# Layer scale on one core: five loads instead of seven, and partitions that own 64 consecutive rows of each half of the tensors

## The chip, the cores and the metric

One core of a Trainium2 chip runs the kernel; the other cores do nothing. The metric is the device time of one execution in microseconds. Executions of one kernel agree within some tenths of a per cent, so the differences of 0.3 us in this study need repeated runs; where a ratio is given, it comes from rounds in which both kernels ran on the same chip (five rounds for each experiment, four to six runs of the kernel in question). All runs quoted were at a granted clock of 1.0.

## The reference

```python
B, S, D = 1024, 16, 512          # x, y: bf16 [1024, 16, 512]; gamma: bf16 [512]
def reference(x, y, gamma):
    return x + gamma * y
```

Flattened, x and y have 16384 rows of 512 bf16, 1 KiB a row and 16 MiB a tensor. Two are read and one is written: 50.33 MB.

## The kernel before

With 128 partitions each partition owns 128 rows. "Row" below means one such row index: 1 KiB in each of 128 partitions, 128 KiB in all. SyncE issues the loads, ScalarE issues gamma and the stores, one small matmul on TensorE spreads gamma over the partitions, VectorE multiplies by gamma and adds x. The kernel keeps all 128 rows of y on chip, but only 77 rows of x, so the last x loads reuse the buffer of rows already added.

```python
PIECES = [40, 37, 40, 11]        # VectorE's pieces, in rows
# loads: (tensor, first row, last row, place in the x buffer); stores 's' of rows 0..64 and 64..128
SP = [('x', 0, 40, 0), ('y', 0, 40), ('x', 40, 77, 40), ('y', 40, 77), ('y', 77, 128),
      ('x', 77, 117, 0), ('x', 117, 128, 40)]
ACT = [('g',), ('s', 0, 64), ('s', 64, 128)]
RELEASE = ('x', 77, 117, 0)      # the stores wait until this load has landed
DVE = [('m', 0), ('a', 0), ('m', 1), ('a', 1), ('m', 2), ('a', 2), ('m', 3), ('a', 3)]
# ... (cut)
xv = xf.rearrange("(p n) d -> p n d", p=P)     # partition p owns rows p*128 .. p*128+127
# ... (cut) in the loop over SP: an x load waits until the adds that read its buffer are done
if need > known:
    eng.wait_ge(s_add, need)
to = x_sb[:, w[3] : w[3] + w[2] - w[1], :]
i = eng.dma_start(out=to, in_=xv[:, w[1] : w[2], :]).then_inc(s_load[w], 16)
# ... (cut) VectorE, per piece c
nc.vector.tensor_tensor(out=yt, in0=yt, in1=g, op=MULT).then_inc(s_dve, 1)
nc.vector.tensor_tensor(out=yt, in0=xt, in1=yt, op=ADD).then_inc(s_add, 1)
```

Of the kernel before, what the change touches and what calls it, by code (L numbers as in the profile page):

```python
# [3 lines left out]


PIECES = [40, 37, 40, 11]



SP = [('x', 0, 40, 0), ('y', 0, 40), ('x', 40, 77, 40), ('y', 40, 77), ('y', 77, 128), ('x', 77, 117, 0), ('x', 117, 128, 40)]  # L10
ACT = [('g',), ('s', 0, 64), ('s', 64, 128)]

EARLY = (2, 1)


RELEASE = ('x', 77, 117, 0)

DVE = [('m', 0), ('a', 0), ('m', 1), ('a', 1), ('m', 2), ('a', 2), ('m', 3), ('a', 3)]
MULT, ADD = mybir.AluOpType.mult, mybir.AluOpType.add


def _take(sem, n, eng):


    return eng.wait_ge(sem, n).then_inc(sem, -n)  # L25


def kernel(
    tc: tile.TileContext,
    x: bass.AP,  # L30
    y: bass.AP,
    gamma: bass.AP,
    out: bass.AP,
):



    nc = tc.nc
    P = nc.NUM_PARTITIONS
    tc.close()  # L40
    tc.compile()  # L41

    xf = x.flatten_outer_dims()
    yf = y.flatten_outer_dims()
    of = out.flatten_outer_dims()
    N, D = xf.shape
    rows = N // P
    n = len(PIECES)
    assert sum(PIECES) == rows
    starts = [sum(PIECES[:c]) for c in range(n + 1)]  # L50
    dt = xf.dtype
    xv = xf.rearrange("(p n) d -> p n d", p=P)
    yv = yf.rearrange("(p n) d -> p n d", p=P)
    ov = of.rearrange("(p n) d -> p n d", p=P)

    gamma_row = nc.alloc_sbuf_tensor("gamma_row", [1, D], dt).ap()
    ones_row = nc.alloc_sbuf_tensor("ones_row", [1, P], dt).ap()
    gamma_sb = nc.alloc_sbuf_tensor("gamma_sb", [P, D], dt).ap()
    y_sb = nc.alloc_sbuf_tensor("y_sb", [P, rows, D], dt).ap()
    x_loads = [w for w in SP + ACT if w[0] == "x"]  # L60
    y_loads = [w for w in SP + ACT if w[0] == "y"]
    stores = [w for w in SP + ACT if w[0] == "s"]
    for loads in (x_loads, y_loads, stores):
        assert sum(w[2] - w[1] for w in loads) == rows
    x_rows = max(w[3] + w[2] - w[1] for w in x_loads)
    x_sb = nc.alloc_sbuf_tensor("x_sb", [P, x_rows, D], dt).ap()
    gamma_ps = nc.alloc_psum_tensor("gamma_ps", [P, D], mybir.dt.float32).ap()

    sem = nc.alloc_semaphore
    s_gamma, s_ones, s_ps, s_dve = sem("s_gamma"), sem("s_ones"), sem("s_ps"), sem("s_dve")  # L70
    s_load = {w: sem("s_" + "_".join(map(str, w[:2]))) for w in x_loads + y_loads}
    s_add, s_go, s_rel, s_end, s_out = sem("s_add"), sem("s_go"), sem("s_rel"), sem("s_end"), sem("s_out")
    added = [a for kind, *a in DVE if kind == "a"]
    order = {a[0]: k for k, a in enumerate(added)}

    def meets(a, b, c, d):
        return a < d and c < b

    def pieces_of(a, b):
        return [c for c in range(n) if meets(starts[c], starts[c + 1], a, b)]  # L80

    def x_at(row):
        return next(w[3] + row - w[1] for w in x_loads if w[1] <= row < w[2])

    def frees(w):

        old = x_loads[: x_loads.index(w)]
        old = [v for v in old if meets(v[3], v[3] + v[2] - v[1], w[3], w[3] + w[2] - w[1])]
        return [c for v in old for c in pieces_of(v[1], v[2])]

    early = []

    def ring(eng, what, n_early):

        known, went = 0, False
        for k, w in enumerate(what):
            kind = w[0]
            need = frees(w) if kind == "x" else pieces_of(w[1], w[2]) + list(w[3:]) if kind == "s" else []
            need = max((order[c] + 1 for c in need), default=0)
            if kind == "s" and not went:  # L100
                _take(s_go, 1, eng)
                went = True
            if need > known:
                eng.wait_ge(s_add, need)
                known = need
            if kind == "g":
                i = eng.dma_start(out=gamma_row, in_=gamma.unsqueeze(0)).then_inc(s_gamma, 16)
            elif kind == "x":
                to = x_sb[:, w[3] : w[3] + w[2] - w[1], :]
                i = eng.dma_start(out=to, in_=xv[:, w[1] : w[2], :]).then_inc(s_load[w], 16)  # L110
            elif kind == "y":
                r = slice(w[1], w[2])
                i = eng.dma_start(out=y_sb[:, r, :], in_=yv[:, r, :]).then_inc(s_load[w], 16)
            else:
                r = slice(w[1], w[2])
                i = eng.dma_start(out=ov[:, r, :], in_=y_sb[:, r, :]).then_inc(s_out, 16)
            if k < n_early:
                early.append(i.ins)

    ring(nc.sync, SP, EARLY[0])  # L120
    ring(nc.scalar, ACT, EARLY[1])


    nc.vector.memset(ones_row, 1.0).then_inc(s_ones, 1)  # L124
    _take(s_ones, 1, nc.tensor)
    _take(s_gamma, 16, nc.tensor)
    nc.tensor.matmul(gamma_ps, ones_row, gamma_row, start=True, stop=True).then_inc(s_ps, 1)  # L127
    _take(s_ps, 1, nc.vector)
    nc.vector.tensor_copy(out=gamma_sb, in_=gamma_ps).then_inc(s_dve, 1)  # L129
    _take(s_dve, 1, nc.vector)  # L130

    _take(s_load[RELEASE], 16, nc.tensor)
    nc.tensor.sem_inc(s_go, 1)
    nc.tensor.sem_inc(s_rel, 1)

    landed, open_mults = set(), 0

    def need(loads, c):
        for w in loads:
            if w not in landed and meets(starts[c], starts[c + 1], w[1], w[2]):  # L140
                if w == RELEASE:
                    _take(s_rel, 1, nc.vector)
                else:
                    _take(s_load[w], 16, nc.vector)
                landed.add(w)

    for kind, *args in DVE:
        c = args[0]
        yt = y_sb[:, starts[c] : starts[c + 1], :]
        if kind == "m":  # L150
            need(y_loads, c)
            g = gamma_sb[:, None, :].to_broadcast([P, PIECES[c], D])
            nc.vector.tensor_tensor(out=yt, in0=yt, in1=g, op=MULT).then_inc(s_dve, 1)  # L153
            open_mults += 1
        else:
            need(x_loads, c)
            if open_mults:
                _take(s_dve, open_mults, nc.vector)
                open_mults = 0
            at = x_at(starts[c])  # L160
            xt = x_sb[:, at : at + PIECES[c], :]
            nc.vector.tensor_tensor(out=yt, in0=xt, in1=yt, op=ADD).then_inc(s_add, 1)  # L162


    nc.scalar.sem_inc(s_end, 1)
    _take(s_end, 1, nc.sync)
    _take(s_add, n, nc.sync)
    _take(s_out, 16 * len(stores), nc.sync)

    main = nc.main_func.blocks[0].instructions  # L170
    names = {i.name for i in early}
    for b in nc.main_func.blocks[1:]:
        for i in [i for i in b.instructions if i.name in names]:
            b.instructions.remove(i)
    for k, i in enumerate(early):
        main.insert(1 + k, i)
# [30 lines left out]
```

## Time and profile before

| | before |
|---|---|
| time, median | 119.99 us (119.98 to 120.29) |
| span in the trace | 118.8 us |
| VectorE busy | 70.2 us (59%) |
| the two DMA queues, share of 16 engines | 66.0% + 32.6% |
| last add ends / second store issued / its first packet | 97.44 / 97.47 / 98.47 us |

The span counts from the first instruction to the last event; the timed run has 1.3 us more around it. (The trace of before is of an execution of 120.14 us, 118.8 of them span; the 1.2 us in the prediction come from setting that span against the median of 119.99.) A DMA of 128 partitions is cut into 128 packets, one a partition, 8 on each of the 16 DMA engines, and each engine ends with a 4-byte packet that counts up the semaphore (145 packets under 512 B on the page: 9 DMAs x 16, and one for gamma). The packet records of the trace give start and duration of each. The lines that carry the reading are in the prediction.

### The profile page before, as it was taken

How to read it: one execution, taken by the hardware profiler on the slowest of the kernel's cores; microseconds unless marked ns; L12 is line 12 of the kernel's file. 1: busy time of each engine (PE TensorE's matmuls, PEld its weight loads, DVE VectorE, ACT ScalarE, POOL GpSimd, SP SyncE). 2: the span in 40 equal slices, each digit the busy share in tenths (PEclk: the TensorE clock that was granted, in tenths of full speed). 3: DMA queues.
4: the chain of work that ended last, by engine and by line, in shares of the span. 5: the costliest groups of instructions: out<-in, count | busy, mean ns of one | idle time of the engine just before them, and what ended most of it. 6: DMA issues, size and time to landing. Idle time of an engine off the chain costs nothing. (4 is left out here: it accounts for less than half of the span.)

```text
span 118.8 us, 84 instructions
## 1 busy us (share of the span) xinstructions
PE 0.6 (0%) x1; PEld 0.1 (0%) x1; DVE 70.2 (59%) x10; POOL 0.2 (0%) x4
## 2 busy tenths in 40 slices
PE   0100000000000000000000000000000000000000
PEld 0000000000000000000000000000000000000000
DVE  0020000009999999799999999999999980000000
POOL 0000000000000000000000000000000000000000
DMA  7999999999999999989696999998899889988890
GB/s 221 442 441 441 441 441 441 441 425 408 408 421 472 485 459 408 475 369 563 281 563 262 441 414 441 408 637 353 353 530 530 353 353 397 662 353 353 353 684 22
DMA packets 1298, 50.33 MB, mean 424 GB/s; under 512 B 145, under 2 KB 146, under 8 KB 146
## 3 DMA queue, kind: packets, MB, share of 16 engines
q1 hardware_dynamic: 1008, 33.55, 66.0%
q10 hardware_dynamic: 290, 16.78, 32.6%
HBM read 33.56 MB, written 16.78 MB: 424 GB/s over the span
## 5 line engine op out<-in xcount | busy, mean ns | idle before, releaser
L153 DVE TENSOR_TENSOR y_sb<-y_sb,gamma_sb 128x20480 bf16<-128x20480 bf16 (+2 forms) x4 | 34.8, 8688 | 20.6 <-DVEq L25 20.6
L162 DVE TENSOR_TENSOR y_sb<-x_sb,y_sb 128x20480 bf16<-128x20480 bf16 (+2 forms) x4 | 34.8, 8691 | 0.6
L129 DVE CAST gamma_sb<-gamma_ps 128x512 bf16<-128x512 f32 x1 | 0.7, 690 | 4.1 <-DVEq L25 4.1
L124 DVE MEMSET ones_row<- 1x128 bf16 x1 | 0.2, 165 | 2.0 <-PEq L41 2.0
L127 PE MATMUL gamma_ps<-gamma_row,ones_row 1*128 1x512 bf16 x1 | 0.6, 581 | 5.5 <-PEq L25 5.5
L127 PEld LDWEIGHTS gamma_ps<-gamma_row,ones_row 1*128 1x128 bf16 x1 | 0.1, 98 | 5.5 <-issue 5.5
L191 POOL MEMSET const-bfloat16-1.0<- 128x1 bf16 x1 | 0.1, 102 | 0.0
L191 POOL MEMSET const-uint8-127<- 128x1 uint8 x1 | 0.1, 101 | 0.0
L191 POOL MEMSET const-float32-0.0<- 128x1 f32 x1 | 0.1, 99 | 0.2 <-issue 0.2
L191 POOL MEMSET const-float32-1.0<- 128x1 f32 x1 | 0.1, 98 | 0.0
## 6 DMA issues: line engine op xcount, KB each, us to landing
x_sb<-in_x_dram SPq DMA_DIRECT2D x2, 5120.0 KB, 21.3
y_sb<-in_y_dram SPq DMA_DIRECT2D x1, 6528.0 KB, 61.8
y_sb<-in_y_dram SPq DMA_DIRECT2D x1, 5120.0 KB, 26.3
x_sb<-in_x_dram SPq DMA_DIRECT2D x1, 4736.0 KB, 36.0
y_sb<-in_y_dram SPq DMA_DIRECT2D x1, 4736.0 KB, 46.9
x_sb<-in_x_dram SPq DMA_DIRECT2D x1, 1408.0 KB, 10.6
out_dram<-y_sb ACTq DMA_DIRECT2D x2, 21.8
gamma_row<-in_gamma_dram ACTq DMA_DIRECT2D x1, 1.0 KB
```

The lines of the kernel that those rows point to most:

```text
L124: nc.vector.memset(ones_row, 1.0).then_inc(s_ones, 1)
L127: nc.tensor.matmul(gamma_ps, ones_row, gamma_row, start=True, stop=True).then_inc(s_ps, 1)
L129: nc.vector.tensor_copy(out=gamma_sb, in_=gamma_ps).then_inc(s_dve, 1)
L153: nc.vector.tensor_tensor(out=yt, in0=yt, in1=g, op=MULT).then_inc(s_dve, 1)
L162: nc.vector.tensor_tensor(out=yt, in0=xt, in1=yt, op=ADD).then_inc(s_add, 1)
L191: nc = _bacc.Bacc("TRN2", target_bir_lowering=False, num_devices=1)
```

## The change

Intent: each full load covers 8 MiB of contiguous memory, there are two loads fewer, and VectorE is done earlier, so that the last store can be issued earlier. Core of the diff:

```diff
-PIECES = [40, 37, 40, 11]
+PIECES = [53, 11, 53, 11]
-SP = [('x', 0, 40, 0), ('y', 0, 40), ('x', 40, 77, 40), ('y', 40, 77), ('y', 77, 128), ('x', 77, 117, 0), ('x', 117, 128, 40)]
+SP = [('y', 0, 64), ('x', 0, 64, 0), ('y', 64, 128), ('x', 64, 117, 0), ('x', 117, 128, 64)]
-RELEASE = ('x', 77, 117, 0)
+RELEASE = ('x', 64, 117, 0)
-DVE = [('m', 0), ('a', 0), ('m', 1), ('a', 1), ('m', 2), ('a', 2), ('m', 3), ('a', 3)]
+DVE = [('m', 0), ('m', 1), ('a', 0), ('a', 1), ('m', 2), ('m', 3), ('a', 2), ('a', 3)]
-    xv = xf.rearrange("(p n) d -> p n d", p=P)
+    xv = xf.rearrange("(c p n) d -> p c n d", p=P, c=2)
     # the same for yv and ov; at(v, a, b) picks the half c and the rows in it
-                i = eng.dma_start(out=to, in_=xv[:, w[1] : w[2], :]).then_inc(s_load[w], 16)
+                i = eng.dma_start(out=to, in_=at(xv, w[1], w[2])).then_inc(s_load[w], 16)
     # ... cut: the same for y and the stores; frees() now looks only at the pieces whose buffer rows overlap
```

More of the change, by code (lines that the diff above doesn't have):

```diff
@@ L51 @@
     dt = xf.dtype
-    xv = xf.rearrange("(p n) d -> p n d", p=P)
-    yv = yf.rearrange("(p n) d -> p n d", p=P)
-    ov = of.rearrange("(p n) d -> p n d", p=P)
+    xv = xf.rearrange("(c p n) d -> p c n d", p=P, c=2)
+    yv = yf.rearrange("(c p n) d -> p c n d", p=P, c=2)
+    ov = of.rearrange("(c p n) d -> p c n d", p=P, c=2)
     gamma_row = nc.alloc_sbuf_tensor("gamma_row", [1, D], dt).ap()
@@ L85, in frees, with at @@
     def frees(w):
-        old = x_loads[: x_loads.index(w)]
-        old = [v for v in old if meets(v[3], v[3] + v[2] - v[1], w[3], w[3] + w[2] - w[1])]
-        return [c for v in old for c in pieces_of(v[1], v[2])]
+        c = set()
+        for v in x_loads[: x_loads.index(w)]:
+            lo, hi = max(v[3], w[3]), min(v[3] + v[2] - v[1], w[3] + w[2] - w[1])
+            if lo < hi:
+                c |= set(pieces_of(v[1] + lo - v[3], v[1] + hi - v[3]))
+        return sorted(c)
+    def at(v, a, b):
+        c = a // (rows // 2)
+        return v[:, c, a - c * (rows // 2) : b - c * (rows // 2), :]
     early = []
@@ L109, in ring @@
                 to = x_sb[:, w[3] : w[3] + w[2] - w[1], :]
-                i = eng.dma_start(out=to, in_=xv[:, w[1] : w[2], :]).then_inc(s_load[w], 16)
+                i = eng.dma_start(out=to, in_=at(xv, w[1], w[2])).then_inc(s_load[w], 16)
             elif kind == "y":
                 r = slice(w[1], w[2])
-                i = eng.dma_start(out=y_sb[:, r, :], in_=yv[:, r, :]).then_inc(s_load[w], 16)
+                i = eng.dma_start(out=y_sb[:, r, :], in_=at(yv, w[1], w[2])).then_inc(s_load[w], 16)
             else:
                 r = slice(w[1], w[2])
-                i = eng.dma_start(out=ov[:, r, :], in_=y_sb[:, r, :]).then_inc(s_out, 16)
+                i = eng.dma_start(out=at(ov, w[1], w[2]), in_=y_sb[:, r, :]).then_inc(s_out, 16)
             if k < n_early:
```

## The prediction

> **What bounds the kernel now.** I first read the page for which unit is busy, then its strip of 40 slices, then the DMA queues, then the timeline for the two places where a DMA waits for VectorE, and at last the single packet records of the trace.
>
> The head of the page, the slices and the DMA queues:
>
> ```profile
> span 118.8 us, 84 instructions
> ...
> PE 0.6 (0%) x1; PEld 0.1 (0%) x1; DVE 70.2 (59%) x10; POOL 0.2 (0%) x4
> ...
> DVE  0020000009999999799999999999999980000000
> ...
> DMA  7999999999999999989696999998899889988890
> ...
> DMA packets 1298, 50.33 MB, mean 424 GB/s; under 512 B 145, under 2 KB 146, under 8 KB 146
> ...
> q1 hardware_dynamic: 1008, 33.55, 66.0%
> q10 hardware_dynamic: 290, 16.78, 32.6%
> ```
>
> VectorE works 59% of the span and nothing in the last 21 us; the two DMA queues (q1 the loads issued by SyncE, q10 gamma and the stores issued by ScalarE) together hold the 16 DMA engines 66.0 + 32.6 = 98.6% of the span. The 6s in the DMA row look like holes, but a packet is counted in the slice where it starts and lasts 1.4 to 2.4 us, so slices of 3 us alias. Summing the packet records in steps of 1 us gives 16.0 of 16 engines busy from 2 us to 117 us, with two exceptions: the first packet starts at 1.00 us, and between 98 and 100 us the sum falls short by 0.29 engine-us, 0.02 us per engine. The last packet ends at 118.46.
>
> The chain of waits the page prints covers 3.2 us of VectorE only, because it does not follow DMAs; it says nothing here. The timeline shows where VectorE could hold up a transfer:
>
> ```profile
> 26.84 10.83 DVE L153 TENSOR_TENSOR y_sb<-y_sb,gamma_sb 128x20480 bf16<-128x20480 bf16 x1 [19.94 <-DVEq L25]
> 37.81 10.82 DVE L162 TENSOR_TENSOR y_sb<-x_sb,y_sb 128x20480 bf16<-128x20480 bf16 x1
> 48.67 21.18 SPq L110 DMA_DIRECT2D x_sb<-in_x_dram  x2
> 49.30 10.03 DVE L153 TENSOR_TENSOR y_sb<-y_sb,gamma_sb 128x18944 bf16<-128x18944 bf16 x1 [0.66 <-DVEq L25]
> ...
> 77.07 20.74 ACTq L116 DMA_DIRECT2D out_dram<-y_sb  x2
> ...
> 94.35 3.09 DVE L162 TENSOR_TENSOR y_sb<-x_sb,y_sb 128x5632 bf16<-128x5632 bf16 x1
> ```
>
> (Start, duration, engine.) The x load of rows 77 to 117 is issued at 48.67, as the first add frees its buffer, but the y load ahead of it in the queue has packets until 64.15: 15 us to spare. The second store is issued at about 77.07 + 20.74 - 0.35 = 97.46, after the last add (94.35 + 3.09 = 97.44); its first packets start at 98.47, where the first store's end. That is the 0.02 us hole: VectorE's end has just no slack, but also costs nothing to speak of. So the bound is the time that 50.33 MB take on 16 DMA engines.
>
> **What the Trainium skill says.** "DMA: Bandwidth & Descriptors", section "Where 436 GB/s comes from", gives 435 GB/s as the ceiling of the 16 ports, 27.2 GB/s each. The trace agrees to the per cent: the median load packet of 40960 B takes 1514 ns (27.05 B/ns), the store packet of 65536 B 2418 ns (27.10 B/ns), 16 times that is 433 GB/s. "HBM Reference", section "Specifications (TRN2)", says a core streaming alone measures about 425 GB/s, bound by its DMA engines; the page above has 424 mean. The first page, section "Latency and other measured facts", warns that row pitches of large powers of two slow HBM (512 KiB and up in its table, with 16 KiB tiles). Here the pitch between partitions falls from 128 rows x 1 KiB = 128 KiB to 64 KiB, so away from the warned side; the trace of before, at 128 KiB, shows no slowing, with load and store packets at the same rate. Nothing yet shows 64 KiB.
>
> **The change, part by part.** It moves the same 50.33 MB. (1) Layout: each partition owns 64 rows in each half, so a full 64-row DMA covers 8 MiB of contiguous HBM, and a load's packet is 65536 B, the size stores already have. (2) Loads fall from 7 to 5, so 2 x 128 = 256 packets fewer, 2 x 8 = 16 per engine. (3) VectorE's pieces become 53, 11, 53, 11 rows with both multiplies ahead of both adds. (4) The first reloaded x buffer waits for the 53-row add, the last x load (11 rows) has a buffer of its own.
>
> Packet cost from medians: 11264 B 422 ns, 37888 B 1401, 40960 B 1514, 52224 B 1928, 65536 B 2418. Between 40960 and 65536 that is 0.03678 ns per byte, leaving 1514 - 40960 x 0.03678 = 7.3 ns fixed. Each engine has 8 packets of every DMA:
> - Before: 8 x (3 x 1514 + 2 x 1401 + 1928 + 422 + 2 x 2418) = 116.24 us.
> - After, with 54272 B (53 rows) worth 1514 + 13312 x 0.03678 = 2004 ns: 8 x (3 x 2418 + 2004 + 422 + 2 x 2418) = 116.13 us.
>
> That is 0.11 us less. Two semaphore packets fewer per engine (about 9 ns each in the trace) give 0.02, and the hole at 98 us, if it closes, 0.02. The start (1.00 us to the first packet, and 0.68 us by which the first 16 packets outlast later ones, 2.19 against 1.51) I keep as it is. Sum: -0.15 us.
>
> Does the queue stay full? DVE durations: 40 rows take 10.82, 11 rows 3.08 us, so 0.267 us a row plus 0.15, and 53 rows take 14.29. DMA data ends at 1.00 + 0.68 + 8 x 2.418 = 21.0 for y of the first half, 40.4 for x, 59.7 for y of the second half, then + 16.0 = 75.8 for the 53 rows of x, + 3.4 = 79.2 for the 11; the engine starts 0.5 us after the data ended, as it did before (26.33 to 26.84). So: multiply 53 at 21.5 to 35.8, multiply 11 to 38.9, add 53 at 40.9 to 55.2, add 11 to 58.3, second multiplies from 60.2 to 74.5 and 77.6, adds to 91.9 and 95.0. The x load that waits for the add is issued at 55.2; at 1.0 us from issue to first packet it is there at 56.3, while the queue has work until 59.7: slack 3.4 us, instead of 15. The last store is issued at 95.1, there at 96.1, while the first store's data run to 79.2 + 19.3 = 98.5: slack 2.4 us, instead of none. The stores are released when the 53 rows have landed (about 76.3) and are there by 77.9 behind 11 rows of x that last until 79.2. No hole in any of the three places. VectorE's 2.4 us earlier end is worth only the 0.02 us.
>
> **The rivals.** *A hole before the x reload.* For it: slack shrinks to 3.4 us. It needs the first add to end 3.4 us late, but VectorE durations of equal form differ by only 3 ns (10821 against 10824). A miss of 1 us beyond the slack would cost 1 us: 121. Chance 3%. *HBM slows with the new layout.* For it: the 16 engines now read at half the distance from each other, in larger runs, and all at once; engines locked in step could meet on the same part of the memory. Against it: before, three load pitches in flight and stores in 64 KiB packets all ran at the port's rate. 2% lower rate in the loads only (77 us) would make 121.4; more than 2% of the total needs 3% on them. Chance of any visible loss 7%. *The first packets stretch with their size.* If the 45% by which they are slow is a rate and not a fixed delay, 2418 x 0.45 = 1.09 instead of 0.68: +0.4, time 120.2. *The earlier end of VectorE shows as time.* The intuition behind the change: 97.44 to 95.0 is 2.4 us off the last store's issue, making 117.6. Against it: the port is busy with the first store then; and no 50.33 MB pass at 433 GB/s in less than 116.1 us, plus 1.7 us of start and 1.2 us that the timed run (119.99) has over the span.
>
> **Range and chances.** 119.99 - 0.15 = 119.84. The three runs of before spread over 0.3 us, the start may add 0.4, a slight HBM effect some more; downward there is little but noise. Range 119.3 to 120.5. Two per cent is 2.4 us: faster would beat the port's rate, 1%; slower needs a real hole or a slowed HBM, 3%.
>
> **What would show it.** Right: packets of 65536 B in the load queue at about 2418 ns, 16 of 16 busy from 2 to 117 us, x reload issued near 55 us, last store near 95 us with landing still near 118.5, 896 data packets of x, y and output. Wrong: load packets well over 2.45 us (HBM), empty engines near 57 to 60 us (reload hole), or first packets near 3.5 us (start).

## The result, and the profile after

The changed kernel takes 120.34 us (median of six, 120.24 to 120.7) against 119.99 us; ratio 1.0028, interval 1.0012 to 1.0043. A ratio is the mean time of one kernel's fast runs over that of the other's of the same rounds, so it is not quite the ratio of the medians quoted. The prediction said 119.84 us in a range of 119.3 to 120.5: the class and the range hold. But the small difference has the other sign: +0.35 us where -0.15 was worked out, and the measured time lies in the range only because the range allowed 0.66 us above the worked-out value for a longer start and a slight HBM effect.

The page of the changed kernel, the same lines as were shown of before:

```profile
span 119.0 us, 78 instructions
...
PE 0.6 (0%) x1; PEld 0.1 (0%) x1; DVE 70.0 (59%) x10; POOL 0.2 (0%) x4
...
DMA  9899888998899888988897979598899889988891
...
DMA packets 1010, 50.33 MB, mean 423 GB/s; under 512 B 113, under 2 KB 114, under 8 KB 114
...
q1 hardware_dynamic: 720, 33.55, 66.0%
q10 hardware_dynamic: 290, 16.78, 32.5%
```

Packets fell from 1298 to 1010 (256 data packets and 32 semaphore packets fewer), bytes are the same, and the DMA engines are as full as they were. Summed over steps of 1 us, the packet records give 15.9 to 16.2 of 16 busy from 2 to 118 us (the records of successive packets overlap a little, hence values over 16): the small hole at 98 us is gone, none has come.

The timeline (start, duration, engine; runs of one kind are merged):

```profile
41.52 17.29 DVE L170 TENSOR_TENSOR y_sb<-x_sb,y_sb 128x27136 bf16<-128x27136 bf16 x2 [2.15 <-DVEq L25]
55.84 0.81 SPq L118 DMA_DIRECT2D x_sb<-in_x_dram  x2
60.76 17.29 DVE L161 TENSOR_TENSOR y_sb<-y_sb,gamma_sb 128x27136 bf16<-128x27136 bf16 x2 [1.94 <-DVEq L25]
77.19 18.68 ACTq L124 DMA_DIRECT2D out_dram<-y_sb  x2
78.19 17.29 DVE L170 TENSOR_TENSOR y_sb<-x_sb,y_sb 128x27136 bf16<-128x27136 bf16 x2
```

VectorE is done at 78.19 + 17.29 = 95.48 us instead of 97.44, and the second store is issued at 95.5, but its first packets start when the first store's last ones end, from 98.61 on. Two microseconds at the end of VectorE have gone into waiting in the queue. The reload of x is issued at 55.84; the data ahead of it last until 59.64 to 60.27.

Where the span grew, by the packet records (duration of the median packet, and mean of all of that size). The two traces are of executions of 120.14 and 120.30 us:

| packets | before | changed |
|---|---|---|
| first 16 of the run, mean | 2191 ns (40960 B; others 1514) | 3090 ns (65536 B; others 2418) |
| store, 65536 B, mean | 2419 ns | 2418 ns |
| first three loads, 65536 B, without the first 16 | - | about 2420 ns |
| 53 rows of x, 54272 B | - | 2004 median, 2038 mean, 2159 largest |
| 11 rows of x, 11264 B | 422 median, 423 mean | 422 median, 427 mean, 658 largest |
| sum of all packets, per engine | 117.16 us | 117.23 us |
| last packets end, first to last engine | 117.80 to 118.46 | 117.93 to 118.62 |

The second load of x is slow in part: (2038 - 2004) x 8 packets = 0.27 us per engine, with slow packets between 61 and 71 us. The trace of before has slow packets too: what lies above the median of each size, the first 16 left out, is 0.16 us per engine there and 0.36 here. These 0.20 us more, less the 0.13 us saved by fewer packets, are the 0.06 us by which the sum of packet time grew. The end of the slowest engine grew by 0.16, as the two executions did; so this pair of traces shows less than half of the 0.35 us between the medians.

### The profile page after: what moved, and what is told of

Its sections match the earlier page's. It is cut to its first block, busy times and chain, and to the rows that moved or that the text cites. A ratio compares the mean times of both kernels' runs of the same rounds, so it can differ in the third digit from the quotient of the medians.

```text
span 119.0 us, 78 instructions
## 1 busy us (share of the span) xinstructions
PE 0.6 (0%) x1; PEld 0.1 (0%) x1; DVE 70.0 (59%) x10; POOL 0.2 (0%) x4
## 2 busy tenths in 40 slices
DMA packets 1010, 50.33 MB, mean 423 GB/s; under 512 B 113, under 2 KB 114, under 8 KB 114
## 5 line engine op out<-in xcount | busy, mean ns | idle before, releaser
L161 DVE TENSOR_TENSOR y_sb<-y_sb,gamma_sb 128x27136 bf16<-128x27136 bf16 (+1 forms) x4 | 34.6, 8688 | 15.5 <-DVEq L25 15.5
L170 DVE TENSOR_TENSOR y_sb<-x_sb,y_sb 128x27136 bf16<-128x27136 bf16 (+1 forms) x4 | 34.6, 8688 | 2.3 <-DVEq L25 2.1
```

## The experiments

Theory: the 16 DMA engines set the time in both kernels; VectorE's order and its earlier end are worth nothing; the 0.35 us come from the loads. Rivals for the 0.35 us: chance of an execution, the layout in memory, the larger pieces, VectorE working on the same on-chip memory. Twelve runs (ten new kernels, and both kernels once more), five rounds each: 1 to 4, 5 to 8, and 9 to 12 on another chip. In each call the kernel before ran beside them (120.03, 119.96 and 120.07 us), so kernels of different calls are compared by their ratios.

**1. The kernel before against itself.** No edit.

> The kernel before, unchanged, timed against itself: ratio 1.000 within 0.002, 119.99 us or so. If the slower load packets (37888 and 52224 bytes at 37 to 43 and 52 to 58 us in the first trace, about 0.11 us per engine in all) belong to the program, they lie at the same times again; if they are chance, they lie elsewhere.

119.97 us, ratio 0.9992 (0.998 to 1.0004). So 0.001 is what nothing looks like. Its slow packets were far fewer than in the first trace (37888 B: 1402 mean; 52224 B: 1930) and mostly at other times: these are chance.

**2. The changed kernel again.** No edit.

> The changed kernel, unchanged: ratio 1.003 as before, if the 0.3 us are real. Theory: the 53-row reload of x (54272-byte packets) is slowed by something of the program, and its packets average about 2038 ns again instead of 2004, at 61 to 68 us. Rival: that was chance in one execution, and the slow packets lie elsewhere or are gone, with the ratio nearer to 1.000.

120.40 us (120.12 to 120.69), ratio 1.0032 (1.0018 to 1.0045): the loss is real and the same in size. The trace, however, was of an execution of 120.12 us, one of the two fastest of six, and it has 2009 ns for the 53-row packets and 433 for the 11-row ones. The expectation of 2038 ns again failed: slow packets come and go from execution to execution.

**3. The changed kernel in the old layout.**

```diff
-    xv = xf.rearrange("(c p n) d -> p c n d", p=P, c=2)    # and yv, ov
+    xv = xf.rearrange("(p n) d -> p n d", p=P)
-        return v[:, c, a - c * (rows // 2) : b - c * (rows // 2), :]
+        return v[:, a:b, :]
```

> The changed kernel's five loads, pieces and VectorE order, but each partition owns 128 consecutive rows as before. Result correct. If the 0.3 us come from the layout in HBM (64 KiB from partition to partition, runs with holes in the 53-row load), this is 0.3 us faster than the changed kernel, ratio 0.999 to the kernel before, and the 54272-byte packets average 2004 to 2010 ns. If they come from the larger pieces or from VectorE, it stays at 1.003. My prediction's arithmetic (fewer packets) said 0.9988 for both.

Correct, 120.01 us, ratio 0.9996 (0.9984 to 1.0008). Five loads, the larger pieces and the new VectorE order together change nothing that five rounds can see; the layout costs (1.0032 - 0.9996) x 120 = 0.43 us, give or take 0.2 by the two intervals. The fastest run of experiment 2 (120.12 us) is slower than the slowest of this one (120.11). The packet figure I had named did not decide: this trace has 2018 ns in the mean for the 53-row packets too, though its run was 120.01 us.

**4. The changed kernel with almost no VectorE.**

```diff
-        yt = y_sb[:, starts[c] : starts[c + 1], :]
+        yt = y_sb[:, starts[c] : starts[c] + 1, :]         # likewise the x operand; gamma broadcast to one row
```

> Wrong result on purpose: every multiply and add works on one row of its piece only, all loads, stores and waits stay. Theory that the DMA engines alone set the time: 120.0 to 120.4 us, within 0.3% of the changed kernel, although VectorE falls from 70 us busy to under 6. If VectorE's reads and writes of the buffers slow the load packets beside them, the slow packets are gone and the time is 0.3 us lower (ratio 0.999 to 1.000). The rival that VectorE's end counts in the time would make it several us faster, which I don't expect.

Wrong on purpose (as it should be), 120.54 us, ratio 1.0037 (1.0024 to 1.005). Its page:

```profile
PE 0.6 (0%) x1; PEld 0.1 (0%) x1; DVE 4.0 (3%) x10; POOL 0.2 (0%) x4
...
q1 hardware_dynamic: 720, 33.55, 66.1%
q10 hardware_dynamic: 290, 16.78, 32.6%
```

VectorE falls from 70.0 to 4.0 us, the queues hold the same shares, and the time stays. So VectorE is neither in the way nor the cause of slow packets: this trace has them at 61 to 66 us as well (53-row packets 2026 ns in the mean), and in this execution also in loads of whole runs, around 40 us (0.12 us per engine).

**5. Only the second half's x loads in the old layout.**

```diff
+    xo = xf.rearrange("(p n) d -> p n d", p=P)
-in_=at(xv, w[1], w[2]))
+in_=at(xv, w[1], w[2]) if w[1] < rows // 2 else xo[:, w[1] : w[2], :])
```

> Wrong result on purpose: the changed kernel with only the two loads of the second half of x (53 and 11 rows) reading as before, 128 KiB from partition to partition; all else in the new layout. The changed kernel is at 1.0032, the same loads in the old layout at 0.9996. If the cost of the new layout sits in these two loads (where the first trace had the slow packets), this is at 0.9996 to 1.001. If it sits in the first three loads or the stores, it stays at 1.002 to 1.004.

Wrong on purpose, 120.02 us, ratio 0.9999 (0.9985 to 1.0013). The whole loss goes with these two loads, 9.8 of the 33.5 MB loaded. Its 53-row packets took 2004 ns, all of them. From 60 to 80 us, the changed kernel's first trace and then this one:

```profile
DMA packets 294, 8.73 MB, mean 437 GB/s; under 512 B 35, under 2 KB 35, under 8 KB 35
```

```profile
DMA packets 298, 8.84 MB, mean 442 GB/s; under 512 B 37, under 2 KB 37, under 8 KB 37
```

The three full loads and the two stores in the new layout cost nothing that five rounds can see. But the slow packets alone don't give the time: this execution, without any in the two loads, took 120.15 us, its engines ending between 117.5 and 118.4 us, while that of experiment 3, with 0.17 us of them per engine, took 120.01.

**6. Only the stores in the new layout.**

```diff
 # on top of experiment 3
-    ov = of.rearrange("(p n) d -> p n d", p=P)
+    ov = of.rearrange("(c p n) d -> p c n d", p=P, c=2)
     # ... cut: the store picks its half of ov
```

> Wrong result on purpose: all loads in the old layout, the two stores in the new one (each 8 MiB in one run). If the new layout costs on the side of the stores, 1.002 to 1.004; if on the side of the loads, 0.9996 as with the old layout throughout. The traces so far have every store packet at 2418 ns in both layouts, so I expect 0.9996.

Wrong on purpose, 120.00 us, ratio 0.9999 (0.9986 to 1.0011): the stores don't care.

**7. Old layout, the first three loads cut in four each (nine loads more).**

```diff
 # on top of experiment 3
-SP = [('y', 0, 64), ('x', 0, 64, 0), ('y', 64, 128), ...
+SP = [('y', r, r + 16) for r in range(0, 64, 16)] + [('x', r, r + 16, r) for r in range(0, 64, 16)] \
+   + [('y', r, r + 16) for r in range(64, 128, 16)] + [...   # the two last x loads as before
```

> Old layout, five loads, but each of the first three cut into four loads of 16 rows: nine more loads, so 72 more packets and 9 more semaphore packets per engine. By the prediction's 7.3 ns a packet and 9 ns a semaphore packet this is 72 x 7.3 + 9 x 9 = 0.61 us more than the old layout with five loads (120.0), 120.6 us, ratio 1.0047. Rival: a load costs more than its packets (some gap between one load and the next), then 121 us or more. Rival: packets cost nothing here, 120.0.

Correct, 120.42 us, ratio 1.0039 (1.0026 to 1.0052). By the ratios that is (1.0039 - 0.9996) x 120 = 0.52 us more than experiment 3, give or take 0.2, where 0.61 was expected. The median packet of 16384 B takes 612 ns, against 16384 x 0.03678 + 7.3 = 610 by the prediction's line; the fixed part is 9.4 ns here instead of 7.3. By the medians, 24 packets of 2418 ns became 96 of 612, 0.72 us more per engine, and nine semaphore packets add 0.08. But the start became shorter: the first 16 packets outlast the later ones by 0.46 us instead of 0.73 in experiment 3, which gives 0.26 back and leaves 0.54. (The sums of all packets in the two traces differ by 0.65 us; both hold chance slow packets.) A load more costs about 0.06 us here (0.52 / 9), or 0.09 in packet time when the start stays; the rivals (a gap between loads, or no cost) fall.

**8. VectorE 6 us late.**

```diff
-('a', 2), ('a', 3)]
+('a', 2), ('d', 0), ('d', 0), ('a', 3)]      # 'd': a multiply of 11 rows on a free part of the x buffer
```

> The changed kernel with two more multiplies of 11 rows (3.1 us each, on a free part of the x buffer) just before the last add; result correct. VectorE ends 6.2 us later. Prediction's slack of the last store was 2.4 us (2.1 to 2.5 by the trace of the changed kernel: last add ends at 95.48, first packets 1.0 later, first store's packets end at 98.6 to 99.3), so 3.7 to 4.1 us of hole: 124.0 to 124.5 us. Rival that VectorE's end counts fully: 126.6. Rival that the slack is larger than 6 us: 120.4.

Correct, 124.27 us, ratio 1.0353 (1.0339 to 1.0367), that is (1.0353 - 1.0032) x 120 = 3.85 us more than the changed kernel. The timeline, then engine busy times and DMA starts in stretches (last two columns: DMA share and GB/s, of packets that start in the stretch):

```profile
92.38 6.33 DVE L159 TENSOR_TENSOR x_sb<-x_sb,gamma_sb 128x5632 bf16<-128x5632 bf16 x2
98.96 3.09 DVE L175 TENSOR_TENSOR y_sb<-x_sb,y_sb 128x5632 bf16<-128x5632 bf16 x1 [0.26 <-DVEq L25]
```

```profile
98.00:99.00 1.00, 0.00 (x0) 0.00 (x0) 0.74 (x2) 0.00 (x0) 1.00 0.01 0
99.00:100.00 1.00, 0.00 (x0) 0.00 (x0) 1.00 (x1) 0.00 (x0) 1.00 0.00 0
100.00:101.00 1.00, 0.00 (x0) 0.00 (x0) 1.00 (x1) 0.00 (x0) 1.00 0.00 0
101.00:102.00 1.00, 0.00 (x0) 0.00 (x0) 1.00 (x1) 0.00 (x0) 1.00 0.00 0
102.00:103.00 1.00, 0.00 (x0) 0.00 (x0) 0.05 (x1) 0.00 (x0) 1.00 1.53 655
```

The last add ends at 98.96 + 3.09 = 102.05, 6.57 us later than 95.48. No data packet starts from 98 until after 102 us: that is the hole. By the packet records the engines finish the first store between 98.5 and 99.7 us, and the second store's first packet starts at 102.93, 0.88 us after the add. 6.57 - 3.85 = 2.7 us of lateness were free. This is the slack the prediction put at 2.4 us.

**9 and 10. One of the two x loads in the old layout, the other in the new.**

```diff
-in_=at(xv, w[1], w[2]))
+in_=xo[:, w[1] : w[2], :] if w == RELEASE else at(xv, w[1], w[2]))     # 9; in 10: if w[1] == 117
```

> Wrong result on purpose: as the changed kernel, with only the 53-row load of x in the old layout; the 11-row load and all else in the new one. The changed kernel is at 1.003, both loads old at 1.000. If the 53-row load carries the cost: 1.000. If the 11-row load does: 1.003. If each its part: 1.0015.

> Wrong result on purpose: the mirror of the run before: only the 11-row load of x in the old layout, the 53-row load in the new one. If the 53-row load carries the cost: 1.003; if the 11-row load does: 1.000.

Their outputs are wrong, which doesn't matter for the times. 120.31 us, ratio 1.0015 (0.9998 to 1.0031), and 120.17 us, ratio 1.0017 (1.0 to 1.0035). Each load seems to carry about half, but the intervals reach from none to nearly all: single runs go from 119.98 (9) or 120.03 (10) up to 120.69 us in both. What is clear is that neither alone frees the kernel of the slow executions, as the two together did (119.99 to 120.15). These two ran on the other chip, without the changed kernel itself beside them; experiment 12 shows that the loss is there on that chip too.

**11. The two x loads packed, without holes.**

```diff
+    half = xf[N // 2 :, :]
+    packed = {64: half[: P * 53, :].rearrange("(p n) d -> p n d", p=P),
+              117: half[P * 53 :, :].rearrange("(p n) d -> p n d", p=P)}
-in_=at(xv, w[1], w[2]))
+in_=packed[w[1]] if w[1] in packed else at(xv, w[1], w[2]))
```

> Wrong result on purpose: as the changed kernel, but the 53-row load reads 128 x 53 consecutive rows without holes (53 KiB from partition to partition) and the 11-row load the 128 x 11 rows behind them. If it is the holes in runs 64 KiB apart that cost: 1.000. If any reading of x from one half of its tensor at this place costs, holes or not: 1.003.

Wrong on purpose, 120.06 us, ratio 1.0000 (0.9989 to 1.0012). The same bytes of the same half of x, taken together, in packets of the same size, at the same time, cost nothing when they lie one behind the other. So it is the pattern of addresses that costs (runs of 53 and of 11 KiB, 64 KiB apart), not the packet size nor the place in the order. In all, the 18 timed runs with both loads in that pattern (the changed kernel, experiments 2 and 4; with 12 they are 23) took 120.12 us or more, and the 20 with both in another pattern (3, 5, 6, 11) 119.91 to 120.30, 17 of them under 120.12 (the kernel before: 119.89 to 120.33).

**12. y too read in 53 and 11 rows.**

```diff
-('y', 64, 128),
+('y', 64, 117), ('y', 117, 128),
```

> Correct result: the changed kernel with the second y load cut into 53 and 11 rows, so that y too is read in runs with holes 64 KiB apart. One more load is 8 x 7.3 + 9 ns = 0.07 us. If runs with holes cost 0.3 to 0.4 us wherever they are read: ratio about 1.006 to 1.007 (120.8). If the cost belongs to the two x loads at their place in the order alone: 1.0035 to 1.004 (120.45).

Correct, 120.47 us, ratio 1.0027 (1.0015 to 1.0039). My theory that such a pattern costs 0.3 to 0.4 us wherever it is read falls: the loss did not grow. In its trace most slow packets sat in y's 11-row load (436 ns in the mean, 0.11 us per engine), some in x's (427 ns), while all 53-row packets of x took 2004. That may be the pattern or chance, as slow packets turn up in the old layout too (experiment 3). Why the losses don't add up is open.

No version beat the kernel before: the best (3, 5, 6 and 11) equal it, and of these only 3 computes the right result.

## Why the prediction was right, point by point

**The bound.** Right, and shown: taking 66 us of work off VectorE (experiment 4) changed the time by nothing, and delaying VectorE (8) cost only what went beyond the slack.

**Fewer packets, -0.15 us.** The cost per byte behind it is right (53 rows: 2004 ns worked out, 2004 in the median), the fixed cost per packet a little low (experiment 7: 9.4 ns instead of 7.3). The time of the whole package without the layout, experiment 3, is 0.9996 of before, -0.05 us, with an interval that reaches from -0.19 to +0.10; so -0.15 fits, but is not shown. Nor is an exact part of such a term shown to arrive at the end: experiment 7 has 0.52 us, give or take 0.2, of the 0.61 expected.

**The start kept as it is.** Right: the first 16 packets outlast the others by 3090 - 2418 = 672 ns, where 0.68 us was carried over from packets of 40960 B. The rival of a start that stretches with the packet, 1.09 us, falls.

**The queue stays full.** Right. The reload was issued at 55.84 (predicted 55.2; the add began when the slowest of the 16 engines had landed, 40.93 + 0.6, and I had counted from the average engine), the last store at 95.5 (95.1), VectorE took 14.29 us for 53 rows (14.29), the slack of the last store was 2.7 us (2.4). The slack of the reload was not tested by a delay; by the trace it was about 2.8 us (55.84 + 1.0 against 59.64), not 3.4. The spread of 3 ns between VectorE's durations, on which the low chance of a hole rested, compares two means; single 40-row instructions of before run from 10816 to 10826 ns, which changes nothing here.

**The new layout costs nothing.** This is the term that was wrong. The prediction argued from the pitch alone, 128 KiB to 64 KiB, costed the 53- and 11-row loads by their size alone (2004 and 422 ns), and named a slowed HBM as a rival at 7%. Its argument against that rival speaks of three load pitches before; but all loads of before have one pitch, 128 KiB, and only run lengths differ. Its sign of a slowed HBM, load packets well over 2.45 us, could not show the loss: the slow packets were of 54272 B and took 2.04 us in the mean. What the runs showed: the pitch is harmless where whole 64 KiB runs are read or written (5), but the two x loads that leave part of each run out cost 0.43 us together. With the -0.15 as worked out that makes +0.28; the two measurements of the changed kernel gave 0.0028 and 0.0032 of 120 us, +0.34 and +0.38, each give or take some 0.17. (The 0.43 is itself taken from the second of them, so this checks the size only roughly.) The rival happened, at a size that the range allowed for.

**What stays open.** Which part of the memory path those loads meet is not shown. It is not VectorE (4), not the packet size (11), not the row range of x (11 reads the same half), and not holes as such: the old layout also leaves holes, 53 of 128 KiB, and costs nothing in time (3), although single slow packets occur there too. Pitch, run length and hole were not varied one by one (say, 53 KiB runs 96 KiB apart), so the rule behind the bad pattern is not known. One trace of one execution shows only that execution's slow packets, so the loss in the timed runs is attributed by substitution, not seen packet by packet.

## What to carry to other kernels

When the DMA engines are full from the second microsecond to the last, judge a change by bytes, packets and holes, and then by the address pattern of each load; an earlier end of an engine is worth only the hole that it closes. Before believing in slack, make the engine late by a known amount and see how much of it arrives. A layout chosen for contiguous transfers is contiguous only for the loads that take whole runs: if a buffer forces partial ones, time those loads in both layouts.

## What the Trainium skill lacked or had wrong

- "DMA: Bandwidth & Descriptors", section "Latency and other measured facts": it names slow row pitches from 512 KiB up. Nothing there covers partial runs at a small pitch: 53 and 11 KiB of every 64 KiB cost 0.43 us on 9.8 MB that take 19.4 us (8 x (2004 + 422) ns), about 2%, while 64 of 64 KiB, 53 and 11 of 128 KiB and the same sizes packed cost nothing that five rounds can see.
- "DMA: Bandwidth & Descriptors", section "Where 436 GB/s comes from": it says of HBM to SBUF that the HBM side, about 358 GB/s, binds. Here one core alone loads at 16 x 65536 B / 2418 ns = 434 GB/s, the ceiling of the ports that the same section gives, by the median packet of the loads of whole runs. So the sentence does not hold for a core alone, as the 425 GB/s in the same paragraph also say.
- No page says how long the first packets of a run take: in these runs the first 16 outlast later ones by 0.58 to 0.68 us at 40960 B (two traces), 0.59 to 0.75 at 65536 B (eleven traces) and 0.46 at 16384 B (one), so more like a fixed delay than a slower rate. The first-byte latency of about 600 ns in the section named first may be the same thing; no run here shows it.
- No page has the cost of one more load from SyncE while the queue is full: about 0.06 us of time, 0.09 of packet time (experiment 7). The fixed cost of about 2 us that "DMA: Bandwidth & Descriptors", section "Anatomy of one DMA — SWDGE (gpsimd) path", gives is for a transfer issued from GpSimd; a lone transfer was not timed here.
